# A fixed order of instructions for an attention and mixture-of-experts kernel, in place of a planner's order

## The chip, the cores and the metric

The kernel runs on one core of one Trainium2 chip. The metric is the device time of one execution in microseconds, given as the median of several runs. The core has five engines that run side by side, each through its own instructions in their order: TensorE (PE, matmul), VectorE (DVE), ScalarE (ACT), GpSimd (POOL), and SyncE (SP), which here only issues DMAs. An instruction waits until what it reads is written and what it overwrites has been read.

## The reference

```python
def _attn_ref(x, state):                    # x (8, 8, 512, 64), state (8, 8, 32, 64)
    scores = scale * np.matmul(x, state.transpose(0, 1, 3, 2))
    ...                                     # softmax over the last dimension: a
    xread = np.matmul(a, state)
    scores2 = scale * np.matmul(state, x.transpose(0, 1, 3, 2))
    ...                                     # softmax: a2
    sread = np.matmul(a2, x)
    return np.concatenate([xread, sread], axis=2)

def _moe_ref(x, w_gate, wq, wk, wv, wo):    # x (8, 544, 512), four experts of width 64
    logits = x @ w_gate                     # the two largest are kept; w is the softmax over them
    ...
    for e in range(E):
        q = x @ wq[e]; k = x @ wk[e]; v = x @ wv[e]
        ...                                 # causal softmax of scale * q @ k^T: a
        ye = a @ v @ wo[e]
        ...                                 # added to out with weight w where e is one of a row's two experts
```

The heads of the first stage are joined to rows of 512 numbers; the second stage is causal attention over 512 + 32 rows of a batch, by two of four experts for each row.

## The kernel before

Eight batches go through the same streams of work. Each fp32 operand of a matmul is split into a high and a low fp16 part (`split`, `hi_lo`, `low`, L538 to L566), and a product is three passes (high by high, high by low, low by high). A split can be done by more than one engine: `st.either` lists the ways.

- `load` (L689): two DMAs of x (`xn`, 512 KB each) and the state rows (`sn`).
- `front(b)` (L707): parts of x (`xh`) and their DMA transposes (`xT`); scores against the state, exponent and normalization (`eb`, `at`); `gs`, the state rows times the weights, so that q, k and v are products of `gs` and `at`; the gate; `kt` and `v`; then `m6`, a mask of which experts a row uses, which PE spreads over partitions (`mt`); and the masked queries `qf` and their parts `qm`.
- `side(b)` (L901): the state's own softmax. Its normalized rows go to the buffer `a2` (one buffer; in the profile `a`), high part by ACT or POOL, low part by DVE or POOL, and by a DMA transpose to `a2t`, twice a batch.
- `probs(b, i)` and `reads(b, i)`: for each of four row tiles the scores (PE, from `qm` and `kt`), maximum `mx`, exponent `p`, parts `ph` (two buffers), DMA transpose `pt`; then the read of `v` (`z`), its parts `zh`, their transpose `z`, the output product `wo_n,z`, ACT's copy `o` and two DMAs of 64 rows to the output.
- `tail(g)`: the state rows of a pair of batches, with a mask `m4` in the place of `m6`; after two pairs, one output product `wo_n,tz` and one DMA of 4x32x512 numbers (256 KB).

None of this runs when it is called: class `Steps` records 2034 steps with what each reads and writes. `plan` then makes an order, always taking the step that can start first, by due times; it also chooses the engine of each split, the buffer of each tile, and how many fill products (matmuls of zeros into a bank about to be used, L477) stand ahead of a PE step where PE would wait. `replay` scores an order with random delays, and `run` tries 12 rounds of forward and backward planning for each of three assumed landing times, then 100 changed copies of the due times, and emits the best (L479 for all but the fills). On SP all DMAs stand in one order; a DMA whose data isn't ready holds those behind it.

Of the kernel before, what the change touches and what calls it, by code (L numbers as in the profile page):

```python
# [26 lines left out]
LN = math.log(2.0 ** 15)  # L27

# [57 lines left out]
class Steps:  # L86
# [7 lines left out]
    FILL = 0.0535  # L94

    KEEP = 3.0
    START, LANDED, TICK = 0.65, 0.93, 10.24 / 3
    LANDS = (1.4, 2.0, 2.6)
    SIGNAL = {"PE": 0.2, "ACT": 0.16, "DVE": 0.14, "POOL": 0.1, "SP": 0.0}

    def __init__(self, nc, sb, psum):
        self.nc, self.pools, self.tags, self.all = nc, {False: sb, True: psum}, {}, []
        self.base, self.scale, self.clock, self.kind, self.lines = 0.0, 1.0, 0.0, "", {}
        self.behind = None
        self.lean = {"DVE": 0.0, "ACT": 0.0, "POOL": 0.0}
        self.patience = dict.fromkeys(("PE", "DVE", "ACT", "POOL", "SP"), 0.0)
# [17 lines left out]
    def step(self, eng, dur, calls, reads, writes, land=0.0, after=None, ways=None, issue=0.0, modes=(None, None)):  # L124
        s = dict(modes=modes, eng=eng, dur=dur, calls=calls, ways=[(*w, self.takes_port(w[0], w[2])) for w in ways or [(eng, dur, calls, 0.0)]], want=self.base + self.scale * self.clock, n=len(self.all),
# [80 lines left out]
    def plan(self, want, ways=None, back=False, until=None):  # L206

        steps = self.all  # L210
        after, before = self.links
        then = before if back else after
        waits = [len(x) for x in (after if back else before)]
        ready = [0.0] * len(steps)
        free = dict.fromkeys(("PE", "DVE", "ACT", "POOL", "SP"), 0.0)
        if not back:
            free.update(SP=0.62, POOL=1.14, DVE=1.5, ACT=1.5, PE=0.94)
        dma_free = 0.0
        mode = None
        port = 0.0  # L220
        counts = []
        open_ = {e: [] for e in free}
        pool = {tag: [(0.0, i) for i in range(len(slots))] for tag, slots in self.tags.items()}
        line = {k: (n[0] - 1 if back else 0) for k, n in self.lines.items()}
        fills = {}
        slot, left, last = {}, {i: b.left for i, b in self.bufs.items()}, {}
        used = self.used

        def opens(n):
            for e in ([steps[n]["ways"][ways[n]][0]] if ways else [w[0] for w in steps[n]["ways"]]):  # L230
                open_[e].append(n)

        for n in range(len(steps)):
            if not waits[n]:
                opens(n)

        def start(n):
            t = ready[n]
            need = {}
            for i in used[n]:  # L240
                if i not in slot:
                    b = self.bufs[i]
                    if line[b.turn[0]] != b.turn[1]:
                        return None
                    need[b.tag] = need.get(b.tag, 0) + 1
            for tag, k in need.items():
                p = pool[tag]
                if len(p) < k:
                    return None
                t = max(t, p[k - 1][0])  # L250
            return t

        def held(way):
            return (free["POOL"] if way[0] == "DVE" else port) if way[4] else 0.0

        order = []
        while len(order) < len(steps):
            best = None
            for e, cand in open_.items():
                now, mine = free[e], []  # L260
                for n in cand:
                    t = start(n)
                    if t is None:
                        continue
                    w = steps[n]["ways"]
                    if ways:
                        t = max(t, now, held(w[ways[n]]))
                    else:
                        cost = {x[0]: max(t, free[x[0]], held(x)) for x in w}
                        if len(w) > 1 and e != min(w, key=lambda x: cost[x[0]] + x[1] + x[3])[0]:  # L270
                            continue
                        t = cost[e]
                    mine.append((t, want[n] + (self.KEEP if e == "PE" and steps[n]["modes"][-1 if back else 0] != mode else 0.0), n))
                if mine:
                    t = min(mine)[0] + self.patience[e]
                    t, _, n = min((m for m in mine if m[0] <= t), key=lambda m: m[1:])
                    if best is None or t < best[0]:
                        best = t, n, e
            if best is None and back:

                short = {self.bufs[i].tag for c in open_.values() for n in c for i in used[n] if i not in slot}
                assert short
                for tag in short:
                    pool[tag].append((max(o[3] for o in order), 0))
                continue
            if best is None:
                return 1e9, order, slot, fills
            t, n, e = best
            s = steps[n]
            for i, w in enumerate(s["ways"]):  # L290
                if n in open_[w[0]]:
                    open_[w[0]].remove(n)
                if w[0] == e:
                    way, dur = i, w[1]
            clear = None
            for i in used[n]:
                if i not in slot:
                    b = self.bufs[i]
                    if b.tag == "bank" and clear is None:
                        clear = pool[b.tag][0][0]  # L300
                    slot[i] = pool[b.tag].pop(0)[1]
                    line[b.turn[0]] += -1 if back else 1
            if e == "PE":
                first, last_ = s["modes"][::-1] if back else s["modes"]
                dur += self.SWITCH * (first != mode)
                mode = last_
            end = t + dur
            if e == "PE" and not back and clear is not None:
                at = max(clear, free["PE"])
                if t - at > 0.5:  # L310
                    fills[n] = 0
                    while True:
                        k = int(at / self.TICK)
                        counts.extend([0.0] * (k + 2 - len(counts)))
                        at += self.FILL * (1.0 if counts[k] >= 3072 else 2.0)
                        if at > t - 0.15:
                            break
                        counts[k + 1] += 128
                        fills[n] += 1
            if e == "PE" and not back:  # L320

                at, work = t, dur
                while True:
                    k = int(at / self.TICK)
                    counts.extend([0.0] * (k + 2 - len(counts)))
                    slow = 1.0 if counts[k] >= 3072 else 2.0
                    m = min(work, ((k + 1) * self.TICK - at) / slow)
                    counts[k + 1] += s["land"] * m / max(dur, 1e-6)
                    at, work = at + m * slow + 1e-9, work - m
                    if work <= 1e-9:  # L330
                        break
                end = at
            free[e] = end
            if e == "DVE" and s["ways"][way][4]:
                port = end
            if e == "SP":
                dma_free = max(dma_free, t + s["issue"] + self.START) + s["land"]
                if s["land"] and dur > s["issue"]:

                    free[e] = max(end, dma_free - min(0.95, s["land"] + 0.12))  # L340
                end = dma_free + self.LAND
            end += self.SIGNAL[e]
            for i in used[n]:
                last[i] = max(last.get(i, 0.0), end)
                left[i] -= 1
                if not left[i]:
                    bisect.insort(pool[self.bufs[i].tag], (last[i], slot[i]))
            for o, done in then[n]:
                waits[o] -= 1
                ready[o] = max(ready[o], end if done else t)  # L350
                if not waits[o]:
                    opens(o)
            order.append((n, way, t, end))
        return max(o[3] for o in order), order, slot, fills

    MORE = dict(PE=0.02, HOLD=0.25, OTHER=0.01, LAND=0.1, SIGNAL=0.02)
    VARY = dict(PE=0.009, HOLD=0.045, OTHER=0.009, LAND=0.12, SIGNAL=0.012)

    def replay(self, plan, seed):
# [9 lines left out]
        for n, way, _, _ in order:  # L371
# [3 lines left out]
            for o, ended in before[n]:  # L375
                t = max(t, done[o] if ended else begin[o])
# [819 lines left out]
```

## Time and profile before

| | |
|---|---|
| device time, median of 3 runs | 332.98 us (331.86 to 334.36) |
| span of the profiled execution | 329.7 us |
| profiled execution's own device time | not given on the page; the median is 3.3 us above the span |
| busy | PE 301.7, DVE 265.6, ACT 212.0, POOL 197.5 us |
| fill products | 248, 15.9 us of PE's busy time |
| DMA moved | 47.72 MB |

The profile is one execution. A row of its groups gives the engine, the operation, output and inputs by tile names (in the profile `p32` is `p`, `a2` is `a`, `m6`, `m4` are `m`), the count, the busy time and the mean in ns, and last the idle time ahead of such instructions with what ended it. A row of the chain gives a start in us, a length and the work; the chain is followed back from the last instruction, at each step to what let it go. A row of a table by stretch gives the length, and each engine's busy time with its instructions in brackets.

### The profile page before, as it was taken

Reading aid. Unit: us, or ns where it says so; the run is one execution under the profiler, and the core shown is the slowest. Engines: PE = TensorE matmul, PEld = TensorE weight load, DVE = VectorE, ACT = ScalarE, POOL = GpSimd, SP = SyncE. Lnnn points to the kernel's source line nnn. Section 1 sums busy time; section 2 is a strip of 40 time slices with the busy share of each in tenths; the row PEclk is TensorE's granted clock in tenths of the full one; section 3 lists DMA queues with packets and bytes.
Section 4 is the critical chain, followed back from the end, with each engine's and each line's share of the span. In section 5 each row is a group of like instructions: output and inputs, shape, how many; then the busy total and the mean of one; then the engine's idle time right before and its main releaser. Section 6 shows DMA issues by size and latency. Waiting matters only on the chain.

```text
span 329.7 us, 10132 instructions
## 1 busy us (share of the span) xinstructions
PE 301.7 (92%) x3906; PEld 201.3 (61%) x3906; DVE 265.6 (81%) x850; ACT 212.0 (64%) x483; POOL 197.5 (60%) x267
## 2 busy tenths in 40 slices
PE   7999599899996999978999997999999999999991
PEld 7786275586454655755456754857546846686750
DVE  3789899999998997995789994998988875894430
ACT  4676697585747859556668874866866756365330
POOL 7044286397864877955868960969965844645400
PEclk9999999999999999999799999999999999999997
DMA  8949909983898999999749898397789867408754
GB/s 192 198 108 164 219 10 166 219 115 66 125 194 196 156 164 154 214 162 233 129 96 148 153 230 116 71 145 156 146 149 188 115 127 119 88 20 171 143 127 95
DMA packets 140712, 47.72 MB, mean 145 GB/s; under 512 B 119672, under 2 KB 136056, under 8 KB 140664
## 3 DMA queue, kind: packets, MB, share of 16 engines
q1 hardware_dynamic: 140664, 47.08, 77.9%
q8 instruction: 30, 0.49, 0.6%
q14 instruction: 18, 0.15, 0.2%
HBM read 11.02 MB, written 8.91 MB: 60 GB/s over the span
## 4 chain that ended last, share of the span: by engine, by line
DVE 37%; PE 27%; ACT 13%; DMA 12%; issue 5%; POOL 4%; SPq 1%; ACTq 0%; DVEq 0%; POOLq 0%
PE bank L479 25%; DVE mx L479 4%; DMA pt<-ph 4%; DVE xh L479 3%; DVE qf L479 3%; DVE gs L479 3%; DVE m L479 3%; DVE a L479 2%; DVE sbm L479 2%; DVE eb L479 2%; DMA p<-in_moe_wo_dram 2%; DVE z L479 2%; ACT xh L479 2%; ACT p L479 2%; DMA xn<-in_x_dram 2%
## 5 line engine op out<-in xcount | busy, mean ns | idle before, releaser
L479 PE MATMUL bank<-kt,qm 64*128 64x128 f16 (+7 forms) x384 | 50.8, 303 | 0.8 <-ACT p L479 0.3
L479 PE MATMUL bank<-v,pt 128*128 128x193 f16 x480 | 44.9, 247 | 2.5 <-DMA pt<-ph 1.3
L479 PE MATMUL bank<-wo_n,z 128*128 128x512 f16 x192 | 45.8, 379 | 0.9 <-DMA z<-zh 0.9
L479 PEld LDWEIGHTS <-pt 128*128 128x128 f16 x480 | 40.2, 98 | 8.0 <-issue 3.2
L479 PE MATMUL bank<-at,gs 128*128 128x512 f16 x192 | 44.6, 379 | 0.0
L479 ACT ACTIVATE p<-bank,mx 128x256 f32<-128x256 f32 (+3 forms) x64 | 31.8, 525 | 15.0 <-DVE mx L479 10.5
L479 POOL TENSOR_TENSOR ph<-p,ph 128x256 f16<-128x256 f32 (+3 forms) x24 | 32.2, 1344 | 9.8 <-ACT ph L479 9.3
L479 PEld LDWEIGHTS <-qm 64*128 64x128 f16 (+1 forms) x384 | 22.3, 96 | 17.4 <-issue 5.1
L479 ACT ACTIVATE o<-bank 128x512 f32<-128x512 f32 x34 | 20.0, 593 | 18.0 <-PE bank L479 17.9
L479 POOL TENSOR_TENSOR qm<-qf,qm 128x512 f16<-128x512 f32 x23 | 26.9, 1187 | 6.2 <-ACT qm L479 4.4
L479 PE MATMUL bank<-gs,at 128*128 128x4 f16 (+1 forms) x384 | 29.9, 218 | 0.7 <-DVE mx L479 0.5
L479 DVE TENSOR_REDUCE mx<-bank 128x1 f32<-128x128 f32 (+3 forms) x64 | 28.2, 475 | 2.5 <-PE bank L479 2.3
L479 PEld LDWEIGHTS <-z 128*128 128x128 f16 x192 | 17.7, 98 | 20.0 <-DMA z<-zh 1.6
L479 PEld LDWEIGHTS <-gs 128*128 128x128 f16 x192 | 17.6, 97 | 19.8 <-issue 1.1
L479 PEld LDWEIGHTS <-at 128*128 128x128 f16 x384 | 23.7, 97 | 5.9 <-issue 1.9
L479 POOL TENSOR_TENSOR zh<-z,zh 128x256 f16<-128x256 f32 x29 | 20.3, 700 | 6.1 <-ACT zh L479 5.6
L479 POOL TENSOR_TENSOR z<-z 128x128 f32<-128x128 f32 x32 | 17.1, 538 | 9.1 <-DVE z L479 4.8
L479 ACT ACTIVATE ph<-p 128x256 f16<-128x256 f32 (+3 forms) x26 | 18.7, 722 | 5.9 <-DMA pt<-ph 5.5
L479 DVE SCALAR_TENSOR_TENSOR xh<-xn,xh 128x512 f16<-128x512 f32 x22 | 18.8, 873 | 4.2 <-ACT xh L479 4.0
L479 ACT ACTIVATE xh<-xn 128x512 f16<-128x512 f32 x32 | 19.1, 626 | 4.5 <-DMA xn<-in_x_dram 4.4
L479 DVE TENSOR_TENSOR qf<-bank,mt 64x512 f32<-64x512 f32 (+1 forms) x32 | 21.1, 684 | 1.1 <-ACT mt L479 0.6
L479 POOL TENSOR_TENSOR eb<-eb,sbm 128x512 f32<-128x512 f32 x14 | 15.0, 1080 | 6.9 <-DVE sbm L479 5.4
(175 smaller groups left out, 677.6 us busy)
## 6 DMA issues: line engine op xcount, KB each, us to landing
xn<-in_x_dram SPq DMA_DIRECT2D x16, 512.0 KB
out_dram<-o SPq DMA_DIRECT2D x64, 128.0 KB
sn<-in_state_dram SPq DMA_DIRECT2D x16, 32.0 KB
p<-in_moe_wo_dram SPq DMA_DIRECT2D x2, 256.0 KB
pt<-ph SPq DMA_TRANSPOSE x32
out_dram<-o SPq DMA_DIRECT2D x2, 256.0 KB
z<-zh SPq DMA_TRANSPOSE x29
xT<-xh SPq DMA_TRANSPOSE x28
```

Of the source, the lines that this page charges most:

```text
L479: f(**{k: v.ap() if isinstance(v, View) else v for k, v in kw.items()})
```

## The change

`plan`, `replay` and the search in `run` are taken out. A table `ORDER` of 2034 entries gives for each step its number, its way (the engine of a split) and, where there are some, the number of fill products ahead of it; a table `SLOTS` gives for each kind of tile the buffer number of each turn. `run` walks through them. The recorded steps and the numbers of buffers are unchanged.

```diff
+ORDER = """
+1.0 0.0 2.0 3.0 4.0 67.0 7.0 8.0 10.0 9.0 11.0 70.0 16.0 12.0 68.0 17.0 13.0.24 69.0 18.0 15.0 21.0 26.0 20.1 22.0 72.0 19.0 27.0 23.0.25 14.0 73.0
...
+SLOTS = {
+    "xn": "0101010101101010",
...
-    def plan(self, want, ways=None, back=False, until=None):
...
-    def replay(self, plan, seed):
...
-    def run(self, rounds, climbs, tries=8):
...
+    def run(self):
+
+        order = [entry.split(".") for entry in ORDER.split()]
+        left = {i: iter(slots) for i, slots in SLOTS.items()}
+        assert len(order) == len(self.all)
+        for entry in order:
+            s = self.all[int(entry[0])]
+            calls = s["ways"][int(entry[1])][2]
+            for b in s["bufs"].values():
+                if b.slot is None:
+                    b.slot = self.tags[b.tag][int(next(left[b.tag])) if b.tag in left else 0]
+            if len(entry) > 2:
+                to = next(kw["out"].buf.slot for _, kw in calls)
+                for _ in range(int(entry[2])):
                     self.nc.tensor.matmul(out=to[:, :128], lhsT=self.zeros, rhs=self.zeros, start=True, stop=True, skip_group_check=True)
-            for f, kw in s["ways"][way][2]:
+            for f, kw in calls:
                 f(**{k: v.ap() if isinstance(v, View) else v for k, v in kw.items()})
-        return mean
...
-    return st.run(CFG['ROUNDS'], CFG['CLIMBS'])
+    st.run()
```

PE's steps are the same 263; its fill products go from 248 to 252. By the choice of ways DVE gets 873 instructions for 852, ACT 451 for 469, POOL 264 for 272. SP issues the same 216 DMAs. The emitting lines are L343 (all) and L341 (fills) in the changed kernel.

Three places show what moves. The first is on DVE, near the middle of the program (fourth batch, and the tail of the second pair of batches). `m_1_182` is the mask `m4` of that tail, `qf_139` the masked queries of the fourth batch. Before:

```order
L479 TENSOR_TENSOR tc_0_193<-bank_83,twg_179 128x4
L479 RECIPROCAL bank_79<-bank_79 128x2
L479 TENSOR_SCALAR m_1_182<-twg_180 128x4
L479 SCALAR_TENSOR_TENSOR a_0_146<-e_0_140,s_0_143,a_0_146 128x512
L479 TENSOR_TENSOR c_2_163<-bank_79,wgt_122 128x6
L479 TENSOR_TENSOR tzr_192<-bank_83,tc_0_193 128x256
L479 TENSOR_TENSOR qf_139<-bank_84,mt_138 64x512
L479 TENSOR_TENSOR qf_139<-bank_84,mt_138 128x512
L479 TENSOR_TENSOR qf_139<-bank_82,mt_138 128x512
L479 TENSOR_TENSOR qf_139<-bank_82,mt_138 64x512
```

And in the changed kernel, where the same `tc` and `tzr` rows and the same four `qf` rows stand in rows 343 to 349:

```order
L343 TENSOR_TENSOR tc_0_193<-bank_83,twg_179 128x4
L343 TENSOR_TENSOR tzr_192<-bank_83,tc_0_193 128x256
L343 SCALAR_TENSOR_TENSOR xt_tail_148<-bank_86,xt_tail_148 64x4x32 x2
L343 TENSOR_TENSOR qf_139<-bank_82,mt_138 128x512
L343 TENSOR_TENSOR qf_139<-bank_81,mt_138 64x512
L343 TENSOR_TENSOR qf_139<-bank_81,mt_138 128x512
L343 TENSOR_TENSOR qf_139<-bank_82,mt_138 64x512
L343 TENSOR_SCALAR bank_79<-bank_79 128x2
L343 RECIPROCAL bank_79<-bank_79 128x2
```

The `qf` rows now stand ahead of the `m4` row, which is row 376 before and row 407 after. On PE the fourth batch's four score steps, with six other steps, so come ahead of the product that reads `m4`.

The second place is on ACT, at the state softmax of the fifth batch. `a_0_146` is the only `a2` buffer, whose second write waits for the DMA transpose of its first; `gs_119` are the evictions that the next products of PE read. Before:

```order
L479 ACTIVATE v_0_104<-bank_86 128x256
L479 ACTIVATE v_0_104<-bank_85 128x256
L479 ACTIVATE a_0_146<-e_0_140,s_0_143 128x512
L479 ACTIVATE o_172<-bank_84 128x512
L479 ACTIVATE at_118<-et_197 128x512
L479 ACTIVATE v_0_104<-bank_82 128x256
L479 ACTIVATE p_1_110<-bank_81,mx_153 128x128
L479 ACTIVATE gs_119<-bank_83 128x512
L479 ACTIVATE gs_119<-bank_79 128x512
```

And in the changed kernel:

```order
L343 ACTIVATE gs_119<-bank_81 128x512
L343 ACTIVATE gs_119<-bank_80 128x260
L343 ACTIVATE gs_119<-bank_85 128x260
L343 ACTIVATE gs_119<-bank_82 128x512
L343 ACTIVATE a_0_146<-e_0_140,s_0_143 128x512
L343 ACTIVATE at_118<-et_197 128x512
L343 ACTIVATE zh_167<-z_1_159 128x256
L343 ACTIVATE o_171<-bank_79 128x512
```

All four `gs` evictions now stand ahead of the second write of `a`, and not behind it.

The third place is the end of SP's order. The rows `64x512` are 128 KB stores of a row tile (two each), `4x32x512` is the 256 KB store of state rows. Before:

```order
L479 DMA out_dram<-o_172 64x512
L479 DMA out_dram<-o_169 64x512
L479 DMA out_dram<-o_170 64x512 x2
L479 DMA out_dram<-o_171 64x512 x2
L479 DMA out_dram<-o_172 64x512 x2
L479 DMA out_dram<-o_169 64x512 x2
L479 DMA out_dram<-o_170 4x32x512
```

And in the changed kernel:

```order
L343 DMA_TRANSPOSE pt_0_151<-ph_150 128x4x128
L343 DMA out_dram<-o_172 64x512 x2
L343 DMA out_dram<-o_169 64x512 x2
L343 DMA out_dram<-o_171 4x32x512
L343 DMA out_dram<-o_170 64x512 x2
L343 DMA out_dram<-o_172 64x512 x2
```

The state rows' store is no longer the last; four 128 KB stores stand behind it. At SP's other end the two state loads `sn` of the first batch stand ahead of its two x loads, where they stood behind them.

More of the change, by code (lines that the diff above doesn't have):

```diff
@@ L1 @@
-import bisect
 import math
-import random
 from contextlib import ExitStack
@@ L27 @@
 LN = math.log(2.0 ** 15)
+ORDER = """
[89 rows of a table added]
+"""
+SLOTS = {
+    "bank": ("012345670132451067235410236754675624310241356740213750643216705210673425012351042304126370421064230751642303425275034127"
+        "650327014563210475610475612340621364107564317042361570423160425730421306421304127530412675340216754316754367135042715304"
+        "2517321647031257640312753142706124706217406172530461735406145327061435270145306217450316274506312745"),
+    "xn": "0101010101101010",
+    "p32": "01210201201201201201201201201201201201201",
+    "bd": "01010101",
+    "xh": "0123012301230123",
+    "mb": "01010101",
+    "sbm": "01010101",
+    "m2": "01010101",
+    "kt": "01201020",
+    "lg": "01010101",
+    "gs1": "010101010101",
+    "gt2": "010101010101",
+    "gt1": "010101010101",
+    "s2": "01010101",
+    "wgt": "01010101",
+    "m6": "01010101",
+    "qm": "01010101",
+    "mx": "01230123012301230123012301230123",
+    "xt_tail": "0101",
+    "ph": "01010101010101010101010101010101",
+    "z32": "01201201201201201201201201201201",
+    "c6": "01201201201201201201201201201201",
+    "zh": "01201201201201201201201201201",
+    "tl": "0101",
+    "z": "01010101010101010101010101010101",
+    "tlg": "0101",
+    "twg": "0101",
+    "o": "0123013201320132130213012301230213",
+    "m4": "0101",
+    "tmt": "0101",
+    "tmx": "0101",
+    "tpt": "0101",
+    "tc4": "0101",
+    "tz": "01",
+}
 class View:
@@ L92 @@
     SWITCH = 0.1
[L94 to L99, printed above, removed]
     def __init__(self, nc, sb, psum):
@@ L105, in __init__ @@
         self.lean = {"DVE": 0.0, "ACT": 0.0, "POOL": 0.0}
-        self.patience = dict.fromkeys(("PE", "DVE", "ACT", "POOL", "SP"), 0.0)
     def buf(self, name, shape, dtype=F32, bufs=1, psum=False, flat=None, use=None):
@@ L124, in step @@
     def step(self, eng, dur, calls, reads, writes, land=0.0, after=None, ways=None, issue=0.0, modes=(None, None)):
-        s = dict(modes=modes, eng=eng, dur=dur, calls=calls, ways=[(*w, self.takes_port(w[0], w[2])) for w in ways or [(eng, dur, calls, 0.0)]], want=self.base + self.scale * self.clock, n=len(self.all),
+        s = dict(group=(self.kind, self.base), modes=modes, eng=eng, dur=dur, calls=calls, ways=[(*w, self.takes_port(w[0], w[2])) for w in ways or [(eng, dur, calls, 0.0)]], want=self.base + self.scale * self.clock, n=len(self.all),
                  after=set(), behind=self.behind if after is None else after,
@@ L204, in graph @@
         return after, before
-    def plan(self, want, ways=None, back=False, until=None):
[L210 to L354, printed above, removed]
@@ L512, in state_read_then_moe_attention @@
     st = Steps(nc, sb, psum)
-    st.patience.update(CFG['PAT'])
     zeros = const.tile([P, P], BF16, name="zeros")
```

109 lines of the change are left out of this document (removed), and 88 rows, old and new, of the table ORDER.

## The prediction

> **What bounds the kernel now.** I read the page's busy line first, then busy time by stretch, then the chain of waits, and only then single waits. The page says that TensorE (PE) is the fullest engine:
>
> ```profile
> PE 301.7 (92%) x3906; PEld 201.3 (61%) x3906; DVE 265.6 (81%) x850; ACT 212.0 (64%) x483; POOL 197.5 (60%) x267
> DVE 37%; PE 27%; ACT 13%; DMA 12%; issue 5%; POOL 4%; SPq 1%; ACTq 0%; DVEq 0%; POOLq 0%
> ```
>
> But the second line, the chain that ended last, holds more DVE than PE. The table by stretch (length, then busy time of PE, weight loads, DVE, ACT, POOL, then PE's clock) shows why; I cut it at 104 and 147 us, where the two products stand that need DVE most (below):
>
> ```profile
> 0.00:20.00 20.00, 17.88 (x364) 15.86 (x372) 12.32 (x31) 10.60 (x23) 5.79 (x42) 1.00 0.91 196
> 20.00:104.00 84.00, 74.85 (x1105) 50.25 (x1090) 79.11 (x245) 58.27 (x135) 51.49 (x61) 1.00 0.80 142
> 104.00:147.00 43.00, 38.64 (x503) 26.22 (x502) 39.50 (x133) 29.94 (x71) 33.81 (x41) 1.00 0.95 169
> 147.00:170.00 23.00, 21.34 (x230) 11.58 (x230) 15.73 (x48) 16.25 (x36) 14.16 (x16) 0.93 0.73 144
> 170.00:200.00 30.00, 29.09 (x334) 18.59 (x332) 27.79 (x92) 21.96 (x52) 22.71 (x26) 1.00 0.99 180
> 200.00:244.00 44.00, 41.91 (x530) 26.82 (x530) 37.99 (x121) 31.90 (x71) 31.59 (x36) 1.00 0.75 127
> 244.00:322.50 78.50, 77.98 (x857) 51.94 (x855) 53.18 (x184) 42.56 (x99) 37.97 (x48) 1.00 0.66 125
> ```
>
> From 20 to 104 us DVE works 79.11 of 84 and PE 74.85: DVE is the bound, with 4.9 us idle. After 244 PE works 77.98 of 78.5 and nothing can be gained there. Between the two lie PE's losses: 4.4 us (104 to 147), 1.7 (147 to 170), 0.9 and 2.1. So the time is a sum of three pieces: DVE's work up to some product of the early batches, PE's work behind that product, and what PE loses behind it. The chain shows the one clear stall:
>
> ```profile
> 149.57 4.81 DMA a2t<-a
> ...
> 155.09 0.58 ACT o L479
> ...
> 157.20 0.60 ACT gs L479
> 158.11 10.18 PE bank L479 x100
> ...
> 244.43 58.00 PE bank L479 x680
> ```
>
> ACT stands still for a DMA transpose because the next write of the only `a2` buffer is queued in ACT's order, with five `v`, `p`, `at`, `o` evictions and the gated-weight evictions `gs` behind it (ACT's timeline):
>
> ```profile
> 154.46 0.72 ACT L479 ACTIVATE a<-e,s 128x512 f16<-128x512 f32 x1 [2.90 <-DMA a2t<-a]
> ```
>
> PE then waits for `gs`, and its clock falls too (DVE's table: length, DVE busy, PE's clock):
>
> ```profile
> 150.00:160.00 10.00, 5.92 (x19) 0.94 1.14 205
> 160.00:170.00 10.00, 6.86 (x25) 0.89 0.31 63
> ```
>
> A clock of 0.94 and 0.89 over 10 us each is 0.6 + 1.1 = 1.7 us of work lost besides the gap.
>
> **The change, part by part.** The sum is made against the profiled execution: span 329.7; the median of the runs, 332.98, lies 3.3 above it, which I carry unchanged.
>
> *The start, +1.0.* SyncE now issues the two state loads `sn` ahead of the first x loads:
>
> ```profile
> 0.73 1.08 SPq L479 DMA_DIRECT2D xn<-in_x_dram  x2
> 1.85 1.98 SPq L479 DMA_DIRECT2D sn<-in_state_dram  x2
> 1.25 5.50 DMA xn<-in_x_dram
> ```
>
> The two take 1.98 us to issue, and the chain begins with that x load, so x can come 2.0 us later. Behind it stand the weights, which PE awaits anyway with fill products; if they set the pace the cost is nothing. Bounds 0 to +2.0, the middle taken.
>
> *DVE's debt, +6.2.* The product that reads `m6` of the third batch (at 105.7 us before) has the same 205 us of PE work behind it in both orders: all but one of the PE steps ahead of it are the same. DVE's work ahead of it grows; its `m` writes stand in row 237 before and row 257 now. What comes ahead, from the DVE groups by form:
>
> ```profile
> L479 DVE SCALAR_TENSOR_TENSOR a<-e,s,a 128x512 f16<-128x512 f32 x11 | 10.9, 988 | 3.1 <-ACT a L479 3.1
> L479 DVE SCALAR_TENSOR_TENSOR xh<-xn,xh 128x512 f16<-128x512 f32 x22 | 18.8, 873 | 4.2 <-ACT xh L479 4.0
> L479 DVE TENSOR_TENSOR z<-bank,c 128x384 f32<-128x384 f32 x32 | 17.7, 553 | 1.1
> L479 DVE RECIPROCAL bank<-bank 128x2 f32<-128x2 f32 x32 | 5.4, 172 | 0.5
> L479 DVE TENSOR_REDUCE tmx<-bank 128x1 f32<-128x512 f32 x4 | 2.7, 687 | 1.8 <-PE bank L479 1.8
> L479 DVE SCALAR_TENSOR_TENSOR v<-bank,v 128x256 f16<-128x256 f32 x32 | 12.9, 414 | 1.9 <-ACT v L479 1.6
> L479 DVE TENSOR_TENSOR eb<-eb,sbm 128x512 f32<-128x512 f32 x2 | 1.3, 688 | 0.0
> ```
>
> Two low parts of `a` that POOL did: 2 x 0.99 = 2.0. One more `xh`: 0.9. Two reads of batch 1, each 0.55 + 0.17 and two small rows of about 0.16: 2.1. The tail's maxima: 0.69 and small rows, 1.1. Two `zh` parts and one `tq`, which DVE never did before: their nearest row of 128x256 is `v`, 0.41 each, 1.2 (from nothing to 0.55 each, the `z` row). Small rows 0.4; away go an `eb` and a `qm` of 0.69 each. Sum 2.0 + 0.9 + 2.1 + 1.1 + 1.2 + 0.4 - 1.4 = 6.3, and 6.2 is taken; bounds 5.0 to 6.7. Nothing hides this where DVE is the bound.
>
> *DVE's early waits, -2.4.* It idled 4.9 us from 20 to 104 us. Another order can give back all of it or none; no row prices it, so half.
>
> *PE's losses behind that product, -7.8.* Between this product and the one that reads `m4` of the second pair of batches (147 us), ten more PE steps now stand: three output products, four score steps of the fourth batch and three value products, since DVE's `qf` rows come earlier (shown above). By the page's groups
>
> ```profile
> L479 PE MATMUL bank<-kt,qm 64*128 64x128 f16 (+7 forms) x384 | 50.8, 303 | 0.8 <-ACT p L479 0.3
> L479 PE MATMUL bank<-wo_n,z 128*128 128x512 f16 x192 | 45.8, 379 | 0.9 <-DMA z<-zh 0.9
> L479 PE MATMUL bank<-gs,at 128*128 128x256 f16 x192 | 23.7, 272 | 0.2 <-ACT p L479 0.2
> ```
>
> each group being 32 steps, that is 4 x 1.59 + 3 x 1.43 + 3 x 0.74 = 12.9 us, so PE has 38.6 + 12.9 = 51.5 us to do there. DVE needs 39.5 + about 4 (four `qf` and the like, less what already came in the debt). PE is covered, and its 4.4 us go. Second, in ACT's order the four `gs` evictions now stand ahead of the `a` that awaits the transpose, so the stall of 147 to 170 holds nothing PE needs: 1.7 idle and 1.7 of clock go. 4.4 + 1.7 + 1.7 = 7.8; bounds 0 (as many new waits) and -11 (the other 0.9 and 2.1 too). What becomes late next is DVE at the `m6` product.
>
> The Trainium skill ("TensorE: Matmul & The Clock Gate", Part 1: The HAM clock gate) says that the clock halves only after an idle window of about 3.4 us. By that rule the 1.7 of clock would not be there to win and this term would be -6.1, the total 328.8. The trace speaks against it: PE's idle time was 1.66 us in all of 147 to 170, and the clock fell all the same.
>
> *The end, -2.9.* The chain ends with ACT's last `o`; SyncE's last row is the 256 KB store of the state rows, and the span ends 6.7 us behind that `o`:
>
> ```profile
> 322.39 0.60 ACT o L479
> 317.99 5.61 SPq L479 DMA_DIRECT2D out_dram<-o  x6
> DMA  9799991000029797899914140022222222100000
> ```
>
> The third line is the DMA engines' busy share in 40 slices of 318 to 330 us. The 128 KB stores end by about 324.6; from 325.8 to 328.5 the last store runs alone at two tenths. Now the state rows' output product stands ahead of the last two `wo_n,z` steps, 2 x 1.43 = 2.9 us sooner, and its store ahead of four 128 KB stores. Bounds: 0 if the state store is still the last to land, -3.9 if the last 128 KB store alone sets the end (324.6 for 328.5).
>
> The Trainium skill ("DMA: Bandwidth & Descriptors", Why a DMA increments its semaphore by 16 and not by 1) gives a copy the largest number of engines up to 16 that divides its slowest dimension: four here, for 4x32x512; the two tenths agree. By it the stores that queue behind on those four engines still end late, and the gain stays under 3.9.
>
> *No cost:* POOL and ACT lose eight and eighteen instructions; both were idle a third of the time. DVE's further growth (873 instructions for 852, some 10 us in all) lies, beyond the 6.2, behind the point where PE is the bound.
>
> Sum: +1.0 + 6.2 - 2.4 - 7.8 - 2.9 = -5.9; span 323.8, time 333.0 - 5.9 = **327.1**.
>
> **The rivals.**
>
> *The debt is not repaid (slower).* If DVE again idles 4.9 us ahead of the third batch's `m6` product, and PE again loses as much behind it, only start, debt and end are left: +1.0 + 6.2 - 2.9 = +4.3, 337.3. It decides once fewer than 4.3 us of the two recovered terms (10.2) come in. For it: 205 us of PE work cannot start before that product. Against it: the cover of 12.9 us just behind it.
>
> *Score to read too close (slower).* In the seventh batch the first read of transposed probabilities stands 4 PE steps behind its scores, where 16 stood: 6.1 us of PE work (three score steps, one mask step) for 21. What lies between is maximum, exponent, split and transpose. Two samples, one in a crowded stretch and one in a free one:
>
> ```profile
> 119.19 0.53 DVE mx L479 x2
> 127.11 3.94 DMA pt<-ph
> 260.74 0.45 DVE L479 TENSOR_REDUCE mx<-bank 128x1 f32<-128x128 f32 x2
> 263.49 3.71 SPq L479 DMA_TRANSPOSE pt<-ph  x2
> ```
>
> The first took 119.19 to 131.05, 11.9 us; the second 2.75 to the issue and, with 3.9 for the transpose, 6.7. At 11.9 the seventh batch would wait 5.8 and the eighth (6.5 us left) 5.4: 327.1 + 11.2 = 338.3. At 6.7 it is 0.8 in all. This is the stretch where PE now runs 58 us without a stop, but DVE is only 68% busy there (53.18 of 78.5), which speaks for the short case.
>
> *Waits only change places (no real change).* With half of the two recovered terms: 7.2 - 5.1 - 2.9 = -0.8, 332.2. For it: new orders stall at new places, and the waits for `pt` and `z` transposes of 4 us stay in the chain.
>
> *More comes in.* DVE's 4.9 all gone and the 3.0 of PE's rest as well: 327.1 - 2.5 - 3.0 = 321.6. That the table does not give what it says is no rival: the rows quoted for SyncE, ACT and DVE stand as it lists them.
>
> **How the numbers follow.** Forecast 0.45, its own range 323 to 331; more comes in 0.10; only changed places 0.25; debt 0.10; reads too close 0.10. A measurement of this kernel tells some 1% from no change, so faster is below 329.65 and slower above 336.3. Of the forecast's 0.45, 0.42 lie below 329.65; of the changed places, 0.06; with the 0.10 that is 0.58. Slower is 0.10 + 0.08 of the two slow cases. The rest, 0.24, lies within 1%. The range 320 to 336 takes in the first three cases with their bounds and leaves out most of the slow ones.
>
> **What would show it.** The first x row of ACT near 6.9 instead of 4.9 (start). DVE 20 to 104 us above 79.1 of 84, and the third batch's `m6` product near 110 (105.7 + 1.0 + 6.2 - 2.4). PE idle 104 to 170 near nothing and its clock at 1.00. No wait of PE for `pt` after 250. The span ending some 4 us behind ACT's last `o`, not 6.7. It is wrong if that `m6` product comes after 113, if PE idles over 8 us behind it, or if `pt` waits stand in the last 70 us.

## The result and the profile after

The changed kernel takes 319.67 us (median of 4 runs, 317.81 to 321.91) where the kernel before takes 332.97 us (331.86 to 334.36): a ratio of 0.962, 95% interval 0.956 to 0.968. It is 13.3 us faster; the forecast was 5.9, and the range ended 0.3 us above the measured time. The profiled execution took 317.81 us with a span of 316.0, so 1.8 us lie around a span (1.7 to 1.9 in every execution on record), not the 3.3 that I carried: with 1.8 the profiled execution before took 331.5 us, 1.5 less than the median. The profiled one after is as far below its own median (1.9), so this hardly touches the comparison. Between the two spans lie 13.7 us.

The page after, busy line and the chain by engine:

```profile
PE 300.2 (95%) x3910; PEld 201.2 (64%) x3910; DVE 271.4 (86%) x871; ACT 205.3 (65%) x465; POOL 188.8 (60%) x259
DVE 41%; PE 36%; DMA 7%; ACT 5%; issue 5%; POOL 3%; SPq 2%; POOLq 0%; ACTq 0%; DVEq 0%
```

PE does the same work in a shorter span, DVE 5.8 us more where I had counted some 10, and DMA fell from 12% of the chain to 7%. Busy time by stretch after, cut as in the prediction, the last one at 311.5 us (length, then PE, weight loads, DVE, ACT, POOL, then PE's clock, the DMA share and GB/s):

```profile
0.00:20.00 20.00, 17.28 (x350) 15.22 (x351) 10.45 (x26) 10.21 (x21) 5.66 (x43) 1.00 0.92 191
20.00:104.00 84.00, 81.11 (x1134) 54.19 (x1131) 82.59 (x259) 60.30 (x139) 54.30 (x67) 1.00 0.81 146
104.00:147.00 43.00, 41.04 (x550) 28.46 (x549) 41.60 (x130) 27.51 (x64) 31.03 (x37) 1.00 0.93 171
147.00:170.00 23.00, 22.14 (x241) 12.19 (x240) 20.35 (x66) 18.40 (x43) 19.00 (x21) 1.00 1.01 182
170.00:200.00 30.00, 28.99 (x420) 18.76 (x419) 27.01 (x92) 21.30 (x48) 16.90 (x21) 1.00 0.96 188
200.00:244.00 44.00, 43.16 (x457) 27.84 (x456) 41.65 (x138) 31.71 (x75) 29.54 (x34) 1.00 0.84 144
244.00:311.50 67.50, 66.44 (x773) 44.56 (x770) 47.74 (x166) 35.39 (x80) 32.40 (x40) 1.00 0.56 110
```

The largest gain is in the second row, where I had expected a loss: PE works 81.11 us of 84 for 74.85 before (7.4 us of fill products in both), and DVE idles 1.4 us for 4.9. PE's clock stays at 1.00 throughout here. Over whole executions it is 0.992 to 1.000 on average in the four runs, and 0.974 to 0.990 in 17 runs of the kernel before (0.989 in its profile); by these I estimate that some 2 of the 13.3 us are clock (each time at half clock costs 1.7, see the end).

The product that reads `m6` of the third batch, on which the sum was built, in PE's timeline before and after (start, length, and in brackets the idle time ahead of it):

```profile
105.68 0.89 PE L479 MATMUL bank<-identh,m 128*64 128x128 f16 x24 [1.36 <-DVE tmx L479]
98.25 0.86 PE L343 MATMUL bank<-identh,m 128*64 128x128 f16 x24
```

It came 7.4 us sooner, where the prediction had it 4.8 later. Up to this product PE was busy for 93.05 us before and 92.86 after, so what went is idle time of PE: 12.6 us before, 5.4 after. DVE's rows that write its mask:

```profile
94.92 2.27 DVE L479 TENSOR_SCALAR m<-wgt 128x12 f16<-128x12 f32 x2
97.89 0.30 DVE L343 TENSOR_SCALAR m<-wgt 128x12 f16<-128x12 f32 x2
```

The mask itself came 1.0 us later (98.19 for 97.19). Before, the product stood 8.5 us behind it; now it starts 0.06 us behind it. And the end: ACT's last `o` after, and the DMA engines' busy share in 40 slices of 304 to 316 us:

```profile
311.34 0.60 ACT o L343
DMA  0001197960297960024130221367999989610000
```

PE ended 7.4 us ahead of the span's end before (318.42 + 3.90, 329.7), and 4.7 after (308.67 + 2.60, 316.0). Split at these two marks the 13.7 us are 7.4 up to the `m6` product, 3.6 from it to PE's end, and 2.7 at the end.

### The profile page after: what moved, and what is told of

It reads as the page before. It is cut to its first block, busy times and chain, and to the rows that moved or that the text cites. A ratio compares the mean times of both kernels' runs of the same rounds, so it can differ in the third digit from the quotient of the medians.

```text
span 316.0 us, 10118 instructions
## 1 busy us (share of the span) xinstructions
PE 300.2 (95%) x3910; PEld 201.2 (64%) x3910; DVE 271.4 (86%) x871; ACT 205.3 (65%) x465; POOL 188.8 (60%) x259
## 4 chain that ended last, share of the span: by engine, by line
DVE 41%; PE 36%; DMA 7%; ACT 5%; issue 5%; POOL 3%; SPq 2%; POOLq 0%; ACTq 0%; DVEq 0%
PE bank L343 35%; DVE mx L343 4%; DVE sbm L343 4%; DVE qf L343 4%; DVE eb L343 3%; DVE m L343 3%; DMA pt<-ph 3%; DVE xh L343 3%; DVE gs L343 2%; DVE mb L343 2%; DVE z L343 2%; DVE v L343 2%; DMA z<-zh 2%; SPq L343 2%; DMA a2t<-a 2%
## 5 line engine op out<-in xcount | busy, mean ns | idle before, releaser
L343 PE MATMUL bank<-kt,qm 64*128 64x128 f16 (+7 forms) x384 | 49.7, 299 | 0.5 <-ACT e L343 0.3
L343 PE MATMUL bank<-v,pt 128*128 128x193 f16 x480 | 45.4, 247 | 1.3 <-DVE tmx L343 0.6
L343 ACT ACTIVATE p<-bank,mx 128x128 f32<-128x128 f32 (+3 forms) x64 | 31.5, 526 | 23.2 <-DVE mx L343 22.7
L343 PE MATMUL bank<-wo_n,z 128*128 128x512 f16 x192 | 45.9, 379 | 0.4 <-DVE qf L343 0.2
L343 PE MATMUL bank<-at,gs 128*128 128x512 f16 x192 | 44.1, 379 | 0.0
L343 PEld LDWEIGHTS <-pt 128*128 128x128 f16 x480 | 39.6, 98 | 6.9 <-DMA pt<-ph 2.9
L343 POOL TENSOR_TENSOR ph<-p,ph 128x512 f16<-128x512 f32 (+3 forms) x23 | 29.9, 1303 | 14.4 <-ACT ph L343 10.3
L343 DVE TENSOR_REDUCE mx<-bank 128x1 f32<-128x128 f32 (+3 forms) x64 | 29.1, 478 | 5.6 <-PE bank L343 5.6
L343 PEld LDWEIGHTS <-qm 64*128 64x128 f16 (+1 forms) x384 | 22.6, 96 | 16.5 <-issue 3.0
L343 PEld LDWEIGHTS <-gs 128*128 128x128 f16 x192 | 17.9, 98 | 20.7 <-issue 0.8
L343 PE MATMUL bank<-gs,at 128*128 128x4 f16 (+1 forms) x384 | 30.8, 218 | 0.2
L343 POOL TENSOR_TENSOR qm<-qf,qm 128x512 f16<-128x512 f32 x24 | 28.7, 1209 | 3.9 <-ACT qm L343 3.8
L343 PEld LDWEIGHTS <-z 128*128 128x128 f16 x192 | 17.7, 98 | 20.6 <-issue 2.7
L343 ACT ACTIVATE o<-bank 128x512 f32<-128x512 f32 x34 | 20.2, 593 | 14.2 <-PE bank L343 13.4
L343 POOL TENSOR_TENSOR eb<-eb,sbm 128x512 f32<-128x512 f32 x15 | 15.9, 1073 | 21.5 <-DVE sbm L343 14.8
L343 PEld LDWEIGHTS <-at 128*128 128x128 f16 x384 | 23.8, 97 | 6.4 <-issue 1.1
L343 POOL TENSOR_TENSOR z<-z 128x128 f32<-128x128 f32 x30 | 14.5, 484 | 19.2 <-DVE z L343 16.0
L343 DVE TENSOR_TENSOR qf<-bank,mt 128x512 f32<-128x512 f32 (+1 forms) x32 | 21.1, 680 | 0.9 <-ACT mt L343 0.5
L343 POOL TENSOR_TENSOR zh<-z,zh 128x256 f16<-128x256 f32 x25 | 17.7, 708 | 6.2 <-ACT zh L343 4.5
L343 ACT ACTIVATE xh<-xn 128x512 f16<-128x512 f32 x32 | 18.9, 624 | 1.9 <-DMA xn<-in_x_dram 1.9
L343 POOL TENSOR_TENSOR at<-et,at 128x512 f16<-128x512 f32 x12 | 14.6, 1217 | 8.2 <-ACT at L343 4.5
L343 ACT ACTIVATE ph<-p 128x256 f16<-128x256 f32 (+3 forms) x23 | 17.0, 746 | 3.1 <-DMA pt<-ph 2.7
```

Of the source, the lines that this page charges most:

```text
L343: f(**{k: v.ap() if isinstance(v, View) else v for k, v in kw.items()})
```

## The experiments

Each run is compared by its ratio to runs of the kernel before that were made beside it (their medians are 331.1 to 332.8 us). The old order can be written as such tables too, with the same instructions in the same order on each engine, so each run is an edit of one of the two tables. The theories: **order** (the new order puts first what PE or its banks wait for), **engines** (the gain is in which engine does a split), and the prediction's own **debt** (DVE's work ahead of the `m6` product counts in full, and that product sets the pace).

| run | us | ratio to before (95%) |
|---|---|---|
| new order, old engines | 330.68 | 0.997 (0.994 to 1.000) |
| old order, new engines | 339.61 | 1.018 (1.012 to 1.023) |
| one stretch of the new order alone | 335.02 | 1.007 (1.003 to 1.010) |
| old, mask of the third batch late | 330.68 | 0.994 (0.991 to 0.998) |
| new, 19 low parts on old engines | 331.78 | 0.996 (0.992 to 1.000) |
| new, the other 69 splits on old engines | 322.44 | 0.971 (0.964 to 0.978) |
| new, tail put back | 323.76 | 0.976 (0.970 to 0.982) |
| new, x loads first | 322.78 | 0.972 (0.967 to 0.977) |
| new, 6 low parts of the state softmax old | 323.86 | 0.977 (0.971 to 0.984) |
| new, 13 low parts of x and weights old | 325.70 | 0.978 (0.973 to 0.982) |
| old order, new engines for the 19 low parts | 333.46 | 1.005 (1.001 to 1.008) |
| old, two `a2` buffers | 331.68 | 1.002 (0.999 to 1.006) |
| new, two `a2` buffers | 321.35 | 0.966 (0.959 to 0.973) |
| new, six idle reductions on DVE | 324.63 | 0.979 (0.975 to 0.984) |
| new, tail put back, store in four | 320.59 | 0.962 (0.958 to 0.967) |
| new, store in four | 319.26 | 0.959 (0.954 to 0.964) |

**The debt: the mask later by 6.5 us of DVE work.** In the old table the two rows that write the mask move:

```diff
 474.0 643.0 644.0
-663.0 664.0
 804.0 550.0 475.0
...
 479.0 899.0 480.0
+663.0 664.0
 552.0 694.0
```

> The old kernel; only the two rows on DVE that write the mask of the third batch stand 6.5 us of DVE work later (at about 103 us, still ahead of the product's time of 105.7). The prediction's step (PE waits for this mask, so DVE work ahead of it counts in full): +6 us, 339 us. Rival (PE comes to that product late for other reasons, the mask lay ready for 8.5 us): no change within 1 us, 332 to 334.

It was no slower: 330.68 us, ratio 0.994. In the old order the mask is not what PE waits for. PE's wait of 1.36 us ahead of the product ends with a later row of DVE:

```profile
105.07 0.56 DVE L479 TENSOR_TENSOR z<-bank,c 128x384 f32<-128x384 f32 x1
```

The profile names `tmx` as the end of this wait, but that row's signal comes at 105.70, after the product's start at 105.68. The signal of this `z` comes at 105.63, and in the run with the mask moved the product again starts 0.04 us behind the same `z`. By the tables of the old order the product writes three PSUM banks, and `z` is the last reader of one of them. So DVE does hold the product there, but by a bank that it reads some twenty rows behind the mask, and a mask that moves within DVE's order changes nothing of that.

POOL's timeline before shows something else beside the mask:

```profile
95.02 2.13 POOL L479 TENSOR_TENSOR ph<-p,ph 128x1024 f16<-128x1024 f32 x1 [0.28 <-ACT ph L479]
```

The two tiny rows of the mask took 2.27 us while POOL ran one instruction of 2.13, and ended with it. With the mask moved:

```profile
95.73 0.88 DVE L341 TENSOR_REDUCE tmx<-bank 128x1 f32<-128x512 f32 x2
95.84 2.14 POOL L341 TENSOR_TENSOR ph<-p,ph 128x1024 f16<-128x1024 f32 x1 [0.28 <-ACT ph L341]
102.01 0.39 DVE L341 TENSOR_SCALAR m<-wgt 128x12 f16<-128x12 f32 x2
104.48 0.89 PE L341 MATMUL bank<-identh,m 128*64 128x128 f16 x24 [1.20 <-DVE tmx L341]
```

The same two rows now take 0.39; beside POOL's instruction stand two reductions that read PSUM, 0.88 us together (the longer has a mean of 687 ns). PE came to the product 1.2 us sooner, though its mask was written 5.2 us later (102.40 for 97.19). A DVE row's time in the profile thus holds the time that POOL keeps it waiting.

**Order or engines.** The change gives 88 splits another engine. Two runs keep the one and undo the other (entry, here one of 88):

```diff
-414.0
+414.1
```

> The new order with the old engine of every split. Theory 'order' (the new order puts first on DVE and ACT what PE or a PSUM bank waits for): it keeps most of the gain, 320 to 324 us. Theory 'engines' (the gain comes from which engine does a split, and from POOL and DVE holding each other up less): at least half of the gain goes, 326 to 333 us.

> The old order with the new engine of every split. Theory 'order': no gain, 331 to 337 us, since DVE gets 21 more instructions (some 6 us of work) at places that were planned without them. Theory 'engines': 322 to 328 us.

Neither theory holds alone. The new order with the old engines keeps 1.8 of the 13 us (1.0 by its ratio), and the new engines in the old order cost 6 to 7 us, more than either theory expected. The two pay only together. Which of the 88 carry it:

> The new order; only the 19 low parts made of one DVE instruction or two POOL ones (of the state softmax, of x and of the weights) get their old engine back. Theory 'pairing, long splits' (a low part takes DVE under 1 us and POOL about 2, and a DMA transpose waits for it, so its engine has to suit its place): most of the 11 us that all old engines cost, 326 to 331 us. Rival 'any split': in proportion to the count (19 of 88 changed splits, other theory of no special kind): 321 to 323 us.

> The new order; the other 69 changed splits (of queries, of reads, of probabilities and the like) get their old engine back, the 19 low parts keep the new one. Theory 'pairing, long splits': little is lost, 320 to 324 us. Rival 'any split': most of the loss is here, 327 to 330 us.

Nearly all of it is in the 19 low parts: with their old engines the new order gives back 12 us (331.78), while the 69 others cost some 3. Of the 19, twelve go from POOL to DVE and seven from DVE to POOL, so DVE makes five more. On POOL a low part is two instructions (POOL's groups by form before), on DVE one:

```profile
L479 POOL TENSOR_TENSOR a<-e,a 128x512 f16<-128x512 f32 x5 | 5.8, 1159 | 0.4
L479 POOL TENSOR_SCALAR e<-e,s 128x512 f32<-128x512 f32 x5 | 3.5, 691 | 0.6 <-ACT a L479 0.6
```

1.16 + 0.69 = 1.85 us, where the DVE row after takes 0.86 (shown below). DVE has less to do with the old engines, and yet waits more; the stretch of 20 to 104 us of that run, and three of the waits of DVE in its first 115 us, each for ACT:

```profile
20.00:104.00 84.00, 76.08 (x1071) 51.61 (x1069) 75.62 (x241) 54.84 (x128) 54.65 (x68) 0.98 0.73 130
DVE v L341 <- ACT v L341: 2.7, 2, 1.9
DVE sbm L341 <- ACT eb L341: 2.6, 2, 1.7
DVE at L341 <- ACT at L341: 2.0, 2, 1.1
```

DVE idles 8.4 us of 84 for 1.4 in the new kernel. The run's chain by engine, and the transposes of x and `a` in it:

```profile
PE 32%; DVE 29%; DMA 16%; POOL 9%; ACT 6%; issue 6%; SPq 1%; POOLq 0%; ACTq 0%; DVEq 0%
30.48 4.37 DMA xT<-xh
56.44 3.26 DMA a2t<-a
92.89 3.44 DMA xT<-xh
134.51 5.07 DMA a2t<-a
176.43 6.21 DMA a2t<-a
261.81 4.83 DMA a2t<-a
```

DMA and POOL are 25% of it, for 10% in the new kernel, in whose chain one such transpose stands (`a2t`, 4.97 us). By the tables POOL makes the low part of the first two of the six alone; the other four are made by DVE, so that these transposes are late through POOL itself is not shown for them. What the run does show is that these 19 choices together were no debt: without them DVE has five low parts less to make, and the kernel is 12 us slower. Which low parts:

> The new order; only the six low parts of the state softmax (five that the change moved from POOL to DVE, one the other way) get their old engine back. All 19 low parts together cost 12 us. Theory 'one buffer' (the low part stands between the two uses of the only a2 buffer, and its 1.85 us on POOL for 0.9 on DVE delays both the transpose and ACT's queue): more than half of it, 326 to 331 us. Rival 'x parts' (the loss is in the low parts of x, which the transposes of x wait for): 320 to 323 us.

> The new order; the 13 low parts of x and of the weights get their old engine back, the six of the state softmax keep the new one. The six alone cost some 5 us, all 19 cost 12. Theory 'sum': about 7 us, 325 to 328 us. Rival 'one chain' (both kinds only matter together): under 3 us, 320 to 322.

The six of the state softmax cost 4 to 5 us (by medians and by ratios), the 13 of x and the weights 5 to 6: both kinds count, and together they make 10 of the 12. The six alone fell between the two theories of their run. The pairing once more, from the other side:

> The old order with the new engine of only the 19 low parts. Theory 'pairing' (an order pays only with the engines it was made for): no gain, 331 to 338 us. Rival 'engines' (these low parts belong on DVE in any order): 321 to 327 us.

333.46 us, ratio 1.005: the same 19 engines bring nothing to the old order, which has DVE do other things there.

**Is DVE the bound at all?** Here DVE gets work that helps nobody:

```diff
+            if int(entry[0]) == 663:
+                for _ in range(6):
+                    self.nc.vector.tensor_reduce(out=self.scr[:, :1], in_=self.scr[:, 1:], axis=AX.X, op=ALU.max)
```

> The new kernel with six reductions of 128x512 numbers, whose result nobody reads, on DVE ahead of the mask of the third batch: 6 x 0.68 = 4.1 us of work. If DVE sets the pace of the first half, as the prediction took it (each us of DVE work ahead of that product counts in full): +4.1 us, 323.8. Rival (PE has other work, DVE's queue catches up): within 1.5 us, 319.5 to 321.

324.63 us, 5.0 more than the new kernel for 4.1 us of work (by the two ratios, 0.979 and 0.962, 5.8 with some 2.6 either way). PE's timeline shows it at once:

```profile
102.17 1.49 PE L344 MATMUL bank<-identh,m 128*64 128x128 f16 x24 [4.09 <-DVE m L344]
```

In the new order PE does wait for this mask, and the product moves from 98.25 to 102.17 with it. PE's clock was also at half from 100.66 to 107.49, and the span is 6.8 us longer than the new kernel's. So DVE's work ahead of this mask costs at least its full length in the new order, as the debt said. What was wrong in the debt is its amount, and that it took the same to be true of the old order.

**One stretch alone.** The old table's first 256 entries stand; then come the new table's entries up to about 108 us of the new kernel's run, then what is left, in the old order, which from entry 827 stands as it did. The first entries that differ:

```diff
 326.0 208.0
-789.0 332.0 347.0 576.0 162.0 1057.0 348.0 349.0
+332.0 333.0 334.0 349.0 347.0 343.0 350.0 348.0
...
```

> The old order up to about 43 us of its run, the new order for the work that PE did from there to about 114 us, and the old order for the rest. By the curve of PE's work against time the new order gained 10 us in this stretch. Theory 'order, local': 321 to 325 us, the gain stays behind. Rival 'the gain is borrowed' (DVE only puts off work that the old rest then has to do): 328 to 333 us. By the prediction's term (DVE's debt less half of its waits) the stretch alone would cost 3.8 us: 337.

335.02 us: slower than either, and none of the three expected times. By the trace PE went from 23 to 85 us of its own work (fills left out) in 66.3 us where the old order takes 71.6 and the new one 63.4, and lost more at the seam. The chain at the seam and PE's timeline there:

```profile
114.61 2.24 DMA out_dram<-o
...
118.77 3.10 DMA a2t<-a
117.90 0.85 PE L341 MATMUL bank<-wn,bd 64*32 64x260 f16 x24 [3.99 <-DVE z L341]
124.13 1.44 PE L341 MATMUL bank<-kt,qm 128*128 128x256 f16 x6 [3.98 <-DVE gs L341]
```

A store and a transpose of `a` stand in the chain there, and PE idles twice for 4 us. Then its clock is at half, from 116.65 to 130.30 us (0.58 from 115 to 125, 0.73 from 125 to 135), after two shorter such times near 42 and 48 us. PE worked for 15 of these 20.5 us, so I estimate a loss of some 8 us, against 1.7 in the profile before. So this run can't say how much of the gain is work put off that only the new order's later part has room for: its seam was planned by nobody, and the clock fell with it.

**The single `a2` buffer.**

```diff
-           TSPAN=1.3, TOFF=1.2, KT=3, p32=3, ph=2, at=1, et=1, gs=1, xh=4, a2=1, o=4, sn=1, qf=1, n_eb=1, n_e2=1,
+           TSPAN=1.3, TOFF=1.2, KT=3, p32=3, ph=2, at=1, et=1, gs=1, xh=4, a2=2, o=4, sn=1, qf=1, n_eb=1, n_e2=1,
```

> The old order and old engines with two a2 buffers in place of one, so that ACT's second write waits for no transpose. By the prediction's term for the stall of 147 to 170 us: its 1.7 us idle and 1.7 us of half clock go, 329.4 us. Rival (the stall only moves, DVE being behind by then): 331 to 333 us.

> The new kernel with two a2 buffers. ACT waits 5.0 us in two pieces for a2t transposes in its profile, and PE idles 1.3 and 0.75 us ahead of products that read a2t. Theory 'one buffer': 317 to 319 us. Rival (the transposes themselves and not the buffer are late): no change, 319 to 320.5 us.

Neither moved (1.002; 0.966 beside 0.962). In the old order the stall that I priced at 3.4 us did go, and PE lost time 20 us later instead; this run's busy time by stretch:

```profile
147.00:170.00 23.00, 21.76 (x248) 12.66 (x248) 19.91 (x56) 18.20 (x40) 17.15 (x17) 1.00 0.92 170
170.00:200.00 30.00, 26.86 (x317) 17.08 (x314) 26.96 (x88) 20.66 (x49) 20.63 (x25) 1.00 0.94 169
```

The clock is 1.00 from 147 to 170, but PE works 26.86 of the next 30 us for 29.09 before.

**The start.**

```diff
-1.0 0.0 2.0 3.0 4.0 67.0
+3.0 4.0 1.0 2.0 0.0 67.0
```

> The new kernel with its first two x loads put back ahead of the two state loads in SyncE's order. The prediction's term for the start: -1.0 us, 318.7 us, from 0 to -2. Rival (PE's order begins with the state rows' transposes, which now come 1 us later): no gain or +1 us, 319.7 to 321.

It is 3.1 us slower (322.78), outside both expectations. In the new kernel ACT's first row is the state rows' `bd`, and with x first it comes 3.1 us later, with all x parts behind it in ACT's order. ACT's timelines, new kernel, x first, and for x itself the kernel before and the new one:

```profile
5.38 0.45 ACT L343 ACTIVATE bd<-bank 128x128 f16<-128x128 f32 x2 [3.37 <-PE bank L343]
8.47 0.45 ACT L341 ACTIVATE bd<-bank 128x128 f16<-128x128 f32 x2 [6.45 <-PE bank L341]
4.90 1.15 ACT L479 ACTIVATE xh<-xn 128x512 f16<-128x512 f32 x2 [2.89 <-DMA xn<-in_x_dram]
6.58 1.15 ACT L343 ACTIVATE xh<-xn 128x512 f16<-128x512 f32 x2 [0.75 <-DMA xn<-in_x_dram]
```

So the first x load does land later for standing second, by 1.7 us, but in the new order x is not what PE and ACT begin with. With x first PE waits 3.12 us for the state rows, and its clock is at half from 8.34 to 11.76 us, which is 1.7 us of work (an estimate) and so part of the 3.1.

**The end.** First the tail put back, then the same with the store in four:

```diff
-1967.0 1951.0 2031.0 1968.0 1953.0
+1967.0 1951.0 1968.0 1953.0
...
-1972.0 2032.0 1973.0 1961.0 2033.0 1974.0
+1972.0 1973.0 1961.0 1974.0
...
-1978.0 1979.0
+1978.0 1979.0 2031.0 2032.0 2033.0
```

```diff
         st.dma(out[(g_ - 1) * NB:(g_ + 1) * NB, S:S + NS, :], o, 0.73)
+        parts = st.all[-1]["ways"][0][2]
+        f = parts[0][0]
+        parts[:] = [(f, dict(out=out[(g_ - 1) * NB + i, S:S + NS, :], in_=o[i * NS:(i + 1) * NS])) for i in range(2 * NB)]
```

> The new kernel, with the state rows' last output product, its copy and its 256 KB store put back to the end of PE's, ACT's and SyncE's orders. The prediction's term for the end: +2.9 us, 322.6 us. Rival (the four engines that this store uses are as late when it stands ahead of four other stores): within 0.7 us of the new kernel, 319 to 320.5.

> The new kernel with the state rows' output at the end of all orders, as in the run with the tail put back, but its 256 KB store made as four stores of 32 rows (64 KB). Theory 'four engines' (the single store is slow because only a quarter of the DMA engines carries it): the 2.9 to 4 us of the tail put back come back, 319.5 to 321 us. Rival 'issue' (three more issues of about 0.6 us at the end): 322 to 324.

> The new kernel with only that store made as four of 32 rows, at its new place. Theory 'four engines': the stores that follow it no longer stand behind it on the same engines, about -1 us, 318.7 us. Rival: they were not held up, or the three more issues cost as much; no change, 319.2 to 320.5.

The tail put back costs 4.1 us (323.76), the four stores give 3.2 of them back (320.59), and at the store's new place they change nothing that can be told (319.26). The last `o` and the DMA share of the last 12 us, first with the single store at the end (span 320.0), then with four (span 319.4):

```profile
312.59 0.60 ACT o L341
DMA  9100000000007969898961314012222222100000
```

```profile
314.76 0.60 ACT o L341
DMA  4979505979400000000004989797996545710000
```

One store runs at two tenths for 2.1 us and the span ends 6.8 us behind ACT's `o`; four run at four tenths and more, and it ends 4.0 behind. So the way this one store is cut costs 2.8 us at the end. That fewer engines carry it fits the two tenths; the view gives the share of all 16 engines, not which of them work.

## Why the prediction was wrong

- **DVE's debt (+6.2), as the time of the `m6` product: failed**, and this is the step that made the size wrong. With the waits (-2.4) and the start (+1.0) it should have put the product 4.8 us later; it came 7.4 sooner. Two things were wrong. First, the sum took the product to start when its mask is there, and carried the 8.5 us between the two, PE's idle time ahead of the product among them, unchanged into the new order: a term put at nothing, with no reason given. In the old order the product waited for a bank that DVE read late; the new order gives it banks that are free before the mask is, and the gap went from 8.5 to 0.06 us. From 20 us up to the product PE idled 10.5 us before and 2.7 after. Second, the debt is too large. DVE's busy time up to the mask's end grew from 86.05 to 87.40 us, by 1.4 and not by 6.2; its idle time fell by 2.2 from 20 us on, near the 2.4 of the sum, and grew by 1.9 at the start. Together that is the 1.0 us by which the mask is later.

  The prices of the debt were means of rows that hold waits for POOL, and these waits change rows with the order. The mask's rows, `xh` and `a` are shorter after (873 and 988 ns before for the last two), `gt` is longer:

```profile
L479 DVE TENSOR_SCALAR m<-wgt 128x12 f16<-128x12 f32 x16 | 5.1, 330 | 0.0
L343 DVE TENSOR_SCALAR m<-wgt 128x12 f16<-128x12 f32 x16 | 2.6, 169 | 0.0
L343 DVE SCALAR_TENSOR_TENSOR xh<-xn,xh 128x512 f16<-128x512 f32 x23 | 16.1, 710 | 1.2 <-ACT xh L343 1.1
L343 DVE SCALAR_TENSOR_TENSOR a<-e,s,a 128x512 f16<-128x512 f32 x15 | 12.9, 861 | 0.6 <-ACT a L343 0.5
L479 DVE SCALAR_TENSOR_TENSOR gt<-gt,gt 128x16 f32<-128x16 f32 x8 | 1.7, 212 | 0.1
L343 DVE SCALAR_TENSOR_TENSOR gt<-gt,gt 128x16 f32<-128x16 f32 x8 | 4.5, 566 | 0.1
```

  Over all rows of DVE, the time above the length of the short rows of the same form is about the same (21 us before, 22 after, 23 in the run with 19 old low parts: estimates from the traces). So DVE is hardly held less in all, and this is not where the 12 us of the low parts are. That they were counted only as work, and not by the waits that end sooner with them, is the other side of the same step.
- **PE's losses behind that product (-7.8): half.** From the product to PE's end 3.6 us were gained. The stall of 147 to 170 (1.66 idle, clock 0.93) is 0.9 idle at 1.00, and 104 to 147 loses 2.0 for 4.4, so the named places did improve by about 5 (the work in them has moved by 7 us); but elsewhere PE lost a little more than before: 244 to its end 1.1 idle for 0.5. The cause given for the stall was not right either: PE's idle pieces there before end with ACT's `o` (0.33), DVE's `mx` (0.99) and ACT's `p` (0.34), none with `gs`. And the run with two buffers shows that one of these stalls is not a cost that can be taken off by itself.
- **The start (+1.0): within its bounds, not a price of this move alone.** ACT's first x row came at 6.58 us (6.9 forecast, 4.90 before), and PE is 0.3 to 0.8 us late when it has done 10 to 25 us of its own work. But in the new order the state loads ahead of x are worth 3 us, since PE and ACT begin with the state rows.
- **The end (-2.9): right.** 2.7 between the spans, 4.1 when the tail is put back alone, and the store in four shows that the single store sets that end.
- **Rivals.** Reads too close to their scores: the chain holds one such transpose,

```profile
268.94 4.55 DMA pt<-ph
```

  but PE idled 1.1 us in its last 67.5, near the short case of 0.8, at most 0.3 at once (for the tail's `tpt`) and not for `pt`. The debt not repaid and the change of places did not happen. "More comes in", at 321.6, was the nearest; its chance of 0.10 was too small, since it was held to what DVE lost and what PE lost behind the product, not to the 10.5 us that PE idled ahead of it.
- **The direction was partly luck.** Faster was forecast because the losses behind the product and the end outweighed a loss ahead of it. Those two brought 6.3 of the 10.7 us forecast; the first part, forecast as 4.8 us lost, was the largest gain.
- **What remains open.** By which waits the 19 low parts are worth 12 us in the new order and nothing in the old one is argued from the chains and not separated by a run, nor is how much of the new stretch's gain is work put off. That the banks of the `m6` product are free sooner is read from the traces and tables; no run gave the old order other banks.

## What to carry to other kernels

Before a moved instruction is priced by what stands ahead of it, look whether its reader starts when it ends: a gap of 8.5 us between a mask and its product means that the mask is not the bound, however full its engine is; look then which row frees the bank that the product writes. Price PE's idle time ahead of the point where the sum begins, too. Price a step that goes from one engine to another by when its result is there, not by busy time alone, and try order and engines together: alone the one brought 1 to 2 us here and the other lost 6 to 7. A stall that one edit removes can come back a few steps later, as it did with two `a2` buffers.

## What the runs showed of the hardware

DVE rows that read SBUF alone were held by POOL's work: two of 0.17 us took 2.27 beside one POOL instruction of 2.13, and 0.39 elsewhere, while two reductions from PSUM beside such an instruction took 0.88 together. The Trainium skill ("SBUF — State Buffer", Terms) says that DVE and GpSimd share a port pair that one of them holds for a whole instruction; the trace agrees. A store of 4x32x512 runs at two tenths of the DMA engines' time, four stores of 32x512 at four tenths and more, and that is 2.8 us at the end of a program. PE's clock in the traces is either full or half, and a time at half lasts 3.41 us or a multiple of it (6.83 and 13.65 occur). Before, one ran from 158.84 to 162.25 us, which costs 1.7 us of work (an estimate), behind 3.41 us in which PE idled for 1.62, in pieces of at most 0.99. Counted in the same steps, four other stretches of 3.41 us before had 1.60 to 1.63 us of idle time and kept the full clock, so idle time alone does not decide it.
